# VectorE's extra work moved between a step's maxima and its masks, and the row sums' transpose moved one step earlier

## Chip, cores and metric

One core of a Trainium2 chip runs the whole kernel. The metric is the device time of one execution in microseconds, as the median of several runs.

## What is computed

Three layers in a row, on 2304 tokens (4 batches of 576) of width 512:

```python
scores = q @ k.T / sqrt(64)                       # 4 batches, 8 heads, 576 x 576
thresh = max(scores) - tau                        # per row
scores = where(scores >= thresh, scores, -1e9)
attn = exp(scores - max(scores)); attn /= sum(attn) + 1e-9
x = (attn @ v) as [2304, 512]
x = ((x @ w_a) * (x @ w_b)) @ w_out               # hidden width 1536; these weights come as float64
h = x @ w_in                                      # hidden width 1024, float64 too
out = layernorm(h * softmax(h)) * g_ln @ w_out2
```

## The kernel before

The kernel has three stages. `attention()` takes about the first 270 us of the trace, `moe1()` and `moe2()` the rest. The change is in `attention()` alone.

**Steps.** Two heads of a batch form a pair; there are 16 pairs. A pair has NS = 9 score tiles of 128 queries by 576 keys: eight for the two heads' four full query blocks, and a ninth for the last 64 queries of both. That makes 144 tiles, taken two at a time in 72 steps (`for m in range(tot // 2 + 6)`, line 474; the last six steps drain the pipeline). So a pair begins every four and a half steps. For each character of the string `PROG` (line 473) a step issues one piece of work. The order is written out by hand, and each engine takes its own instructions in the order in which they are issued:

- `A`, `B`: `score()` of the step's first and second tile. TensorE computes the scores into PSUM (line 332; two buffers `ps`). VectorE copies them out, negated and scaled, with their row maxima (line 337, "maxima" below). ScalarE takes the exponentials (line 349).
- `t`, `u`: the tile's threshold, a tiny operation of GpSimd (line 354).
- `V`: TensorE's products with the values (line 414).
- `F`: `finish()` of a pair. TensorE transposes the reciprocal row sums into PSUM (line 435, tile `rt`), and ScalarE copies them out (line 440, tile `zt`).
- `T`, `U`: transposes of the two tiles of the step before (line 383), which ScalarE copies out of PSUM (line 376).
- `Y`: transposes of last keys, that is of keys 512 to 575 (lines 399 and 402, tile `tq`). They exist only in two steps of a pair.
- `X`: in step 72 alone, the first products of the next stage.
- `a`, `b`: the masks of the two tiles, on VectorE (line 363). A mask needs the tile's exponentials and threshold.
- `f`, `z`: `fill()`, VectorE's extra work.

The tiles `rt`, `tp` (of `T` and `U`) and `tq` share one set of three PSUM buffers. A buffer is free when ScalarE has copied it out. ScalarE's copies are issued at the end of the step, behind the step's exponentials; those of `xp` and `zt` come first, then those of the transposes, then the conversion's.

**Extra work.** While attention runs, float64 weights are converted. A weight group has three pieces, and FW = 5 groups (15 pieces) may be converted before attention ends. A piece has six operations: an exponent on ScalarE (line 128); `low`, `sign` and `join` on VectorE (lines 132, 135, 138); a copy on ScalarE (line 142) and a difference on GpSimd (line 145). `fill()` issues one VectorE operation at a time; ScalarE's and GpSimd's are issued at the step's end (line 554). `conv_at` (line 472) lists the steps that may do this: the even ones from 6, and all from 72. If a pair's two operations on row sums (lines 369 and 370) are queued in `lo_old`, `fill()` takes these instead. From step 37, odd steps also issue one VectorE operation that prepares the next stage's input (`x_slots`, lines 228 and 234), eight in all.

Of the kernel before, what the change touches and what calls it, by code (L numbers as in the profile page):

```python
# [21 lines left out]
def kernel(  # L22
# [42 lines left out]
    NS = 2 * NQ + 1  # L65
# [83 lines left out]
    def conv_emit(stage, engs, count=1):  # L149
        while count and conv["k"] < min(conv["ld"], conv["lim"]):  # L150
            if not conv["ops"]:
                conv["ops"] = conv_ops(stage)
            if conv["ops"][0][0] not in engs:
                return
            conv["ops"].pop(0)[1]()
            count -= 1
            if not conv["ops"]:
                conv["k"] += 1
# [24 lines left out]
    def load_x(j):  # L183
        n = LEN[j]
        xr = xr_p.tile([P, KC, NB], F32, name="xr0")[:, :, 0:n]
        zr = xr_p.tile([P, KC, NB], F32, name="zr")[:, :, 0:n]
        for b, s0, m, c in BLK[j]:
            nc.sync.dma_start(out=xr[:, :, c:c + m], in_=xd[b][:, :, s0:s0 + m])
            if b not in vs:
                vs[b] = const.tile([P, KC, 2], F32, name=f"vs{b}")  # L190
                nc.sync.dma_start(out=vs[b], in_=xd[b][:, :, S:S + 2])
                vnew.append(b)
            for h in range(2):
                zs = rzd[b].rearrange("(k h) s -> h k s", h=2)[h:h + 1, :, s0:s0 + m]
                nc.sync.dma_start(out=zr[h * D:(h + 1) * D, :, c:c + m], in_=zs.to_broadcast([D, KC, m]))
        xs[j] = (xr, zr, xhs[j % 2].tile([P, KC, 2, NB], F32R, name="xt")[:, :, :, 0:n])
# [22 lines left out]
    def prep_slots(j):  # L219
        xr, zr, xt = xs[j]  # L220

        def norm(e):
            while vnew:
                b = vnew.pop()
                nc.vector.tensor_scalar(out=vs[b], in0=vs[b], scalar1=neg, scalar2=EPS / S, op0=ALU.mult, op1=ALU.mult)
            for b, _, m, o in BLK[j]:
                xe = xr[:, e, o:o + m]
                nc.vector.scalar_tensor_tensor(out=xe, in0=xe, scalar=vs[b][:, e, 0:1], in1=zr[:, e, o:o + m], op0=ALU.add, op1=ALU.mult)

        def high(e):  # L230
            nc.scalar.activation(out=xt[:, e, 0, :], in_=xr[:, e], func=AF.Copy)

        def low(e):
            nc.vector.tensor_tensor(out=xt[:, e, 1, :], in0=xr[:, e], in1=xt[:, e, 0, :].bitcast(F32), op=ALU.subtract)
            if e == KC - 1:
                later.append(lambda: nc.sync.dma_start(out=xsd[j], in_=xr))
                xs[j] = xt

        slots = []
        for c in range(0, KC, 2):  # L240
            slots += [(lambda e=e: norm(e), lambda e=e: high(e)) for e in range(c, c + 2)]
            slots += [(lambda e=e: low(e), None) for e in range(c, c + 2)]
        return slots
# [35 lines left out]
    def attention():  # L279
# [21 lines left out]
        def alloc_qk(i):  # L301
            q = pq.tile([P, 2, S], F32, name="q")
            k = pq.tile([P, 2, HS + D], F32, name="k")
            ld[i] = (q, k)
# [100 lines left out]
        def pv(i, r, half):  # L405
            n = R1 if r == 1 else R2 + 2
            if half == 0:
                st[i, "o", r] = ps_a.tile([P, 512], F32, name="po", bufs=1)
            po = st[i, "o", r][:, 0:n]
            vr, vt = ld[i, "v"], vz[i % 3]  # L410

            def mm(kc, h):
                lhsT, rhs = (vr[:, h * NQ + kc], dt[h, r][:, kc, 0:n]) if kc < NQ else (vt[:, h], dt["t", r][:, 0:n])
                nc.tensor.matmul(po[h * D:(h + 1) * D], lhsT=lhsT, rhs=rhs, start=(kc == 0), stop=(kc == NQ), skip_group_check=True)  # L414

            def store():
                b, hp = divmod(i, NPAIR)
                if r == 1:
                    st[i, "x"] = px.tile([P, S + 2], F32, name="xp")
                xp = st[i, "x"]  # L420
                c0 = 0 if r == 1 else R1
                nc.scalar.activation(out=xp[:, c0:c0 + n], in_=po, func=AF.Copy)
                if r == 2:
                    dma_q.append(lambda: nc.sync.dma_start(out=xd[b][:, hp, :], in_=xp))

            if half == 1:
                pv_q.append(store)
            cut = NQ // 2
            return [lambda kc=kc, h=h: mm(kc, h) for kc in (range(cut) if half == 0 else range(cut, NQ + 1)) for h in range(2)]
# [31 lines left out]
        tot = NP * NS  # L461

        def fill(n):
            for _ in range(n):
                if lo_old:
                    lo_old.pop(0)()
                elif m in conv_at:
                    conv_emit(wstage, "D")
                    if m >= tot // 2:
                        conv_emit(wstage, "APD", 2)  # L470

        conv_at = [x for x in range(6, tot // 2 + 6) if x % 2 == 0 or x >= tot // 2]
        PROG = 'ABtVFTUYXaufbz'
        for m in range(tot // 2 + 6):
            if m == 30:
                load_x(0)
                x_slots = prep_slots(0)
            cur = [divmod(n, NS) for n in (2 * m, 2 * m + 1) if n < tot]
            old = [divmod(n, NS) for n in (2 * m - 2, 2 * m - 1) if 0 <= n < tot]
            lo_old, lo_q = lo_q, []  # L480
            pvs = [(j,) + PV[j % 2][m - j * NS // 2] for j in range(max(0, 2 * m // NS - 2), min(NP, 2 * m // NS + 1)) if m - j * NS // 2 in PV[j % 2]]
            mms = [f for p in pvs for f in pv(*p)]
            nm = {}
            th = {}

            def score(k):
                if k < len(cur):
                    nm[k] = sm.tile([P, 1], F32, name="nm")
                    scores(*cur[k])
                    soft_max(*cur[k], nm[k])  # L490
                    soft_exp(*cur[k])

            def thr(k):
                if k < len(cur):
                    th[k] = soft_thr(nm[k])

            def mask(k):
                if k < len(cur):
                    soft_mask(*cur[k], th[k])
                    if cur[k][1] == NS - 1:  # L500
                        recip(cur[k][0])

            def turn(k):
                if k < len(old):
                    tpose(*old[k])

            for ch in PROG:
                if ch in "AB":
                    score("AB".index(ch))
                elif ch == "V":  # L510
                    for mm in mms:
                        mm()
                elif ch == "F":
                    for j in range(NP):
                        if m - j * NS // 2 == 9:
                            finish(j)
                elif ch in "TU":
                    turn("TU".index(ch))
                elif ch == "Y":
                    for c in old:  # L520
                        tpose_tail(*c)
                elif ch in "tu":
                    thr("tu".index(ch))
                elif ch in "ab":
                    mask("ab".index(ch))
                elif ch == "f":
                    fill(1)
                elif ch == "X":
                    if m == tot // 2:
                        pre[0, 0] = ab_mm(0, 0)  # L530
                elif ch == "z":
                    fill(max(1, len(lo_old)))
                    if m >= 37 and m % 2 and x_slots:
                        norm_low, high = x_slots.pop(0)
                        norm_low()
                        if high:
                            evac_q.append(high)
            for fn in dma_q + later:
                fn()
            dma_q.clear()  # L540
            later.clear()
            i, s = divmod(2 * m, NS)
            r = m - (i * NS + 1) // 2
            if i < NP and r == 0:
                load_v(i)
                if i + 2 < NP:
                    alloc_qk(i + 2)
                    load_k(i + 2)
                    load_q(i + 2)
            for fn in pv_q + evac_q:  # L550
                fn()
            evac_q, pv_q = [], []
            if m in conv_at:
                conv_emit(wstage, "AP", 3)
                conv_load(wstage)
# [300 lines left out]
```

## Time and profile before

| | us |
|---|---|
| median of 3 runs | 943.42 (943.14 to 944.04) |
| the profiled execution, its own time | 945.94 |
| its span, first to last instruction | 944.1 |

| engine | busy us | share of the span |
|---|---|---|
| TensorE, matmuls (PE) | 921.9 | 98% |
| TensorE, weight loads (PEld) | 704.0 | 75% |
| VectorE (DVE) | 542.4 | 57% |
| ScalarE (ACT) | 440.4 | 47% |
| GpSimd (POOL) | 192.6 | 20% |

The shares are means over three unlike stages. During attention VectorE and ScalarE are busy for 80 to 90% of the time, later for less than half. TensorE's matmuls are pipelined, and the ends of their rows are modelled, so that a busy TensorE may still have small gaps. TensorE's granted clock is full throughout.

### The profile page before, as it was taken

To read this page: it belongs to the slowest core of one execution; us is meant where nothing else is said; L and a number is where in the kernel's file an instruction comes from. 1 tells how busy PE (TensorE), PEld (TensorE's weight loads), DVE (VectorE), ACT (ScalarE), POOL (GpSimd) and SP (SyncE) were. 2 spreads that over 40 slices of the span, in tenths; PEclk is the share of its full clock that TensorE was granted. 3 is DMA by queue.
4 is the path that set the end of the run, shared out by engine and by line. 5 is a ranking of instruction groups with operands and counts; after the bars stand their busy time and mean duration, and the time that the engine had idled before them with its cause. 6 is when DMAs were issued, how large, how long until landed. Compare 5 with 4: busy or idle time off the path is not lost.

```text
span 944.1 us, 15070 instructions
## 1 busy us (share of the span) xinstructions
PE 921.9 (98%) x5680; PEld 704.0 (75%) x5680; DVE 542.4 (57%) x1169; ACT 440.4 (47%) x795; POOL 192.6 (20%) x292
## 2 busy tenths in 40 slices
PE   7999999999999999999999999999999999999998
PEld 3555555555567878889888888889988788888886
DVE  6898989999975754323147772222265544444443
ACT  5788887878763442213235432121232433333332
POOL 1111221212121220000013330000023433333330
PEclk9999999999999999999999999999999999999999
DMA  6443743463135474142115642022052111111100
GB/s 180 126 128 112 206 147 90 124 186 113 51 116 157 155 202 112 45 112 115 65 33 177 211 160 71 19 92 87 24 178 89 34 45 45 45 45 45 45 23 34
DMA packets 52616, 95.46 MB, mean 101 GB/s; under 512 B 12736, under 2 KB 28736, under 8 KB 49984
## 3 DMA queue, kind: packets, MB, share of 16 engines
q1 hardware_dynamic: 52112, 93.91, 32.1%
q8 instruction: 45, 0.74, 0.3%
q10 hardware_dynamic: 432, 0.59, 0.2%
q14 instruction: 27, 0.22, 0.1%
HBM read 70.80 MB, written 23.68 MB: 100 GB/s over the span
## 4 chain that ended last, share of the span: by engine, by line
PE 60%; DVE 3%; DMA 3%; ACT 2%; issue 1%; SPq 0%; POOL 0%; ACTq 0%; DVEq 0%
PE ps L256 26%; PE py L612 14%; PE po L754 10%; PE ps L698 9%; DMA wraw<-in_w_dram 2%; PE pl L735 2%; DVE g L596 1%; ACT gt L597 0%; DVE e L710 0%; DVE w L138 0%; ACT e L709 0%; DVE nm L706 0%; DVE xr L211 0%; ACT w L128 0%; ACT a L595 0%
## 5 line engine op out<-in xcount | busy, mean ns | idle before, releaser
L256 PE MATMUL ps<-xt,w 128*128 128x512 f32 (+1 forms) x1440 | 305.8, 368 | 1.9 <-DVE g L596 1.9
L256 PEld LDWEIGHTS ps<-xt,w 128*128 128x128 f32 x1440 | 251.4, 189 | 47.2 <-DVE g L596 2.3
L145 POOL TENSOR_TENSOR w<-w,w 128x512 fp32r<-128x512 f32 x52 | 76.8, 1478 | 413.5 <-ACT w L142 413.5
L612 PE MATMUL py<-gt,w 128*128 128x512 f32 (+1 forms) x720 | 157.5, 368 | 2.1 <-ACT y L616 2.1
L612 PEld LDWEIGHTS py<-gt,w 128*128 128x128 f32 x720 | 126.2, 189 | 25.0 <-ACT y L616 2.5
L596 DVE TENSOR_TENSOR g<-ps,a 128x512 f32<-128x512 f32 (+1 forms) x60 | 38.3, 638 | 180.7 <-ACT a L595 180.6
L349 ACT ACTIVATE pe<-ns,nm 128x576 f32<-128x576 f32 x128 | 94.0, 775 | 48.3 <-DVE ns L337 48.1
L595 ACT ACTIVATE a<-ps 128x512 f32<-128x512 f32 (+1 forms) x60 | 33.1, 552 | 178.2 <-PE ps L256 175.4
L363 DVE SCALAR_TENSOR_TENSOR pe<-ns,th,pe 128x576 f32<-128x576 f32 x128 | 102.7, 815 | 16.7 <-ACT pe L349 12.5
L337 DVE TENSOR_SCALAR_CACHE_REDUCE ns<-ps 128x576 f32<-128x576 f32 x144 | 102.7, 750 | 7.9 <-PE ps L332 7.8
L698 PE MATMUL ps<-w,ys 128*128 128x512 f32 x432 | 102.6, 393 | 1.6 <-POOL ys L575 1.4
L754 PE MATMUL po<-w,lt 128*128 128x512 f32 x432 | 101.4, 390 | 0.7 <-POOL lt L741 0.6
L332 PE MATMUL ps<-k,q 64*64 64x288 f32 x1152 | 91.2, 424 | 4.7 <-DMA k<-in_qkv_dram 4.4
L754 PEld LDWEIGHTS po<-w,lt 128*128 128x128 f32 x432 | 80.8, 188 | 18.1 <-POOL lt L741 1.1
L698 PEld LDWEIGHTS ps<-w,ys 128*128 128x128 f32 x432 | 79.8, 188 | 18.1 <-POOL ys L575 1.8
L414 PE MATMUL po<-pt,vr 128*64 128x322 f32 (+1 forms) x512 | 78.0, 419 | 1.7 <-ACT pt L376 0.9
L376 ACT ACTIVATE pt<-tp 128x512 f32<-128x512 f32 (+1 forms) x160 | 77.9, 545 | 0.2
L354 POOL TENSOR_SCALAR th<-nm,toff 128x1 f32<-128x1 f32 x144 | 38.4, 269 | 187.8 <-DVE ns L337 187.8
L383 PEld LDWEIGHTS tp<-ident,pe 128*128 128x128 f32 x512 | 55.9, 141 | 24.9 <-issue 9.4
L383 PE MATMUL tp<-ident,pe 128*128 128x128 f32 x512 | 70.9, 278 | 1.1 <-ACT pt L376 0.6
L414 PEld LDWEIGHTS po<-pt,vr 128*64 128x64 f32 x512 | 32.7, 136 | 42.5 <-issue 17.2
L332 PEld LDWEIGHTS ps<-k,q 64*64 64x64 f32 x1152 | 36.8, 134 | 32.8 <-DVE ns L337 7.8
(76 smaller groups left out, 807.6 us busy)
## 6 DMA issues: line engine op xcount, KB each, us to landing
wraw<-in_w_dram SPq DMA_DIRECT2D x36, 512.0 KB, 3.7
q<-in_qkv_dram SPq DMA_DIRECT2D x15, 576.0 KB, 4.1
k<-in_qkv_dram SPq DMA_DIRECT2D x30, 176.0 KB, 4.7
xd<-xp SPq DMA_DIRECT2D x16, 289.0 KB, 2.1
y<-yd SPq DMA_DIRECT2D x18, 256.0 KB, 3.0
vr<-in_v_dram SPq DMA_DIRECT2D x16, 256.0 KB, 3.7
xr<-xd SPq DMA_DIRECT2D x4, 1024.0 KB
zr<-rzd SPq DMA_DIRECT2D x8, 512.0 KB, 9.5
```

The lines of the kernel that those rows point to most:

```text
L145: nc.gpsimd.tensor_tensor(out=w["o"][1], in0=w["f"] if wide else raw, in1=w["o"][0].bitcast(F32), op=ALU.subtract)
L256: nc.tensor.matmul(pa[:, 0:n], lhsT=wt[:, m, wi, kc * P:(kc + 1) * P], rhs=xt[:, kc, xi, :], start=(k == 0), stop=(k == 3 * KC - 1))
L332: nc.tensor.matmul(ps[t * D:(t + 1) * D, g, 0:HS], lhsT=q[r, u, c], rhs=k[r, u, o:o + HS], start=True, stop=True, skip_group_check=True)
L337: nc.vector.tensor_scalar(out=ns, in0=st[i, s][:, :, 0:HS], scalar1=-SCALE, scalar2=None, op0=ALU.mult, op1=ALU.min, accum_out=nm)
L349: nc.scalar.activation(out=pe.rearrange("p (g s) -> p g s", g=2), in_=ns, func=AF.Exp, bias=nm, scale=-1.0)
L363: nc.vector.scalar_tensor_tensor(out=pv, in0=ns, scalar=th, in1=pv, op0=ALU.is_le, op1=ALU.mult, accum_out=z[:, s:s + 1])
L376: evac_q.append(lambda: nc.scalar.activation(out=out, in_=in_, func=AF.Copy))
L383: nc.tensor.transpose(tp[:, kc, :], pe[:, o:o + P], ident)
L414: nc.tensor.matmul(po[h * D:(h + 1) * D], lhsT=lhsT, rhs=rhs, start=(kc == 0), stop=(kc == NQ), skip_group_check=True)
L612: nc.tensor.matmul(py, lhsT=wt[:, 2, wi, oc * P:(oc + 1) * P], rhs=gt[:, gi, :], start=(first and k == 0), stop=(last and k == 2))
L698: nc.tensor.matmul(ph[:, g, :], lhsT=y[:, a, kc, :], rhs=w2(2 * kc + g, b), start=(k == 0), stop=(k == 3 * KC - 1))
L754: nc.tensor.matmul(po, lhsT=lt[:, a, j, :], rhs=w2(2 * KC + j, b), start=(k == 0), stop=(k == 3 * NJ - 1))
```

## The change

The thresholds `t` and `u` are issued together, ahead of `V`. The order `a` `u` `f` `b` `z` at the step's end becomes `f` `a` `b`: one place for VectorE's extra work, after both maxima and ahead of both masks. There a step issues all that is queued on row sums, and then one operation more: the preparation of the next stage's input where it has one, else one of the conversion. Conversion is allowed in every step from 6. `finish()` runs 8 steps after its pair began, and not 9.

```diff
-        conv_at = [x for x in range(6, tot // 2 + 6) if x % 2 == 0 or x >= tot // 2]
-        PROG = 'ABtVFTUYXaufbz'
+        conv_at = range(6, tot // 2 + 6)
+        PROG = 'ABtuVFTUYXfab'
...
                     for j in range(NP):
-                        if m - j * NS // 2 == 9:
+                        if m - j * NS // 2 == 8:
                             finish(j)
...
-                elif ch == "f":
-                    fill(1)
...
-                elif ch == "z":
-                    fill(max(1, len(lo_old)))
+                elif ch == "f":
+                    fill(len(lo_old))
                     if m >= 37 and m % 2 and x_slots:
                         norm_low, high = x_slots.pop(0)
                         norm_low()
                         if high:
                             evac_q.append(high)
+                    else:
+                        fill(1)
```

## Rows read from the trace of the kernel before

**Rows 1.** Page, section 1: busy us of each engine over the whole span.
```profile
PE 921.9 (98%) x5680; PEld 704.0 (75%) x5680; DVE 542.4 (57%) x1169; ACT 440.4 (47%) x795; POOL 192.6 (20%) x292
```

**Rows 2.** Steps 7 to 70: length, then busy us of PE, PEld, DVE, ACT, POOL; clock.
```profile
30.05:266.97 236.92, 231.12 (x2237) 134.07 (x2236) 215.22 (x587) 191.43 (x371) 47.57 (x139) 1.00 0.43 128
```

**Rows 3.** Timeline (start us, length us), VectorE, steps 65 and 66.
```profile
246.13 0.75 DVE L337 TENSOR_SCALAR_CACHE_REDUCE ns<-ps 128x576 f32<-128x576 f32 x1
...
246.81 0.75 DVE L337 TENSOR_SCALAR_CACHE_REDUCE ns<-ps 128x576 f32<-128x576 f32 x1
...
247.81 0.82 DVE L363 SCALAR_TENSOR_TENSOR pe<-ns,th,pe 128x576 f32<-128x576 f32 x1 [0.23 <-POOL th L354]
...
249.29 0.76 DVE L337 TENSOR_SCALAR_CACHE_REDUCE ns<-ps 128x576 f32<-128x576 f32 x1
...
251.72 0.42 DVE L132 TENSOR_SCALAR wlow<-wraw 128x512 uint32<-128x512 uint32 x1
252.05 0.81 DVE L363 SCALAR_TENSOR_TENSOR pe<-ns,th,pe 128x576 f32<-128x576 f32 x1
...
252.79 0.80 DVE L135 SCALAR_TENSOR_TENSOR wlow<-wraw,wlow 128x512 uint32<-128x512 uint32 x1
253.51 0.75 DVE L337 TENSOR_SCALAR_CACHE_REDUCE ns<-ps 128x576 f32<-128x576 f32 x1
```

**Rows 4.** Timeline, TensorE's matmuls, in step 63 and in step 65.
```profile
239.48 0.60 PE L383 MATMUL tp<-ident,pet 128*128 128x128 f32 x4
240.95 0.44 PE L399 MATMUL tq<-ident,pe 128*128 128x128 f32 x2 [0.87 <-ACT zt L440]
...
246.11 1.09 PE L383 MATMUL tp<-ident,pe 128*128 128x128 f32 x8
247.04 0.38 PE L399 MATMUL tq<-ident,pe 128*128 128x128 f32 x2
247.35 1.20 PE L332 MATMUL ps<-k,q 64*64 64x288 f32 x16
```

**Rows 5.** Waits from 27 to 272 us: total us, times, longest.
```profile
DVE pe L363 <- ACT pe L349: 11.5, 49, 0.2
...
PEld tq L399 <- ACT zt L440: 5.5, 6, 1.6
...
PEld ps L332 <- DVE ns L337: 4.8, 18, 0.5
DVE ns L337 <- PE ps L332: 4.8, 7, 0.7
...
PE tq L399 <- ACT zt L440: 4.1, 5, 1.4
```

**Rows 6.** Timeline, TensorE's weight loads ahead of the value products, steps 51 and 67.
```profile
193.51 1.01 PEld L414 LDWEIGHTS po<-pt,vr 128*64 128x64 f32 x8 [1.11 <-ACT pt L376]
...
252.41 0.63 PEld L414 LDWEIGHTS po<-pt,vr 128*64 128x64 f32 x8 [0.44 <-ACT pt L376]
```

**Rows 7.** Groups of VectorE's instructions from 27 to 272 us: busy us, mean ns.
```profile
L138 DVE SCALAR_TENSOR_TENSOR w<-w,wlow 128x512 uint32<-128x512 uint32 x12 | 8.2, 687 | 0.0
...
L370 DVE RECIPROCAL rz<-rz 128x9 f32<-128x9 f32 x16 | 3.4, 210 | 0.0
L228 DVE SCALAR_TENSOR_TENSOR xr<-xr,vs,zr 128x512 f32<-128x512 f32 x4 | 2.9, 735 | 0.0
```

**Rows 8.** Timeline: GpSimd's differences and VectorE's operations near them.
```profile
246.22 1.29 POOL L145 TENSOR_TENSOR w<-w,w 128x512 fp32r<-128x512 f32 x1 [1.98 <-ACT w L142]
...
266.97 0.76 DVE L337 TENSOR_SCALAR_CACHE_REDUCE ns<-ps 128x576 f32<-128x576 f32 x1
267.66 1.28 POOL L145 TENSOR_TENSOR w<-w,w 128x512 fp32r<-128x512 f32 x1 [2.67 <-ACT w L142]
...
276.61 1.30 POOL L145 TENSOR_TENSOR w<-w,w 128x512 fp32r<-128x512 f32 x1 [1.29 <-ACT w L142]
276.73 1.47 DVE L132 TENSOR_SCALAR wlow<-wraw 128x512 uint32<-128x512 uint32 x1 [0.86 <-DMA wraw<-in_w_dram]
```

**Rows 9.** Timeline, ScalarE's first copy of the stage after attention.
```profile
284.39 0.60 ACT L595 ACTIVATE a<-ps 128x512 f32<-128x512 f32 x1 [2.79 <-DMA rzd<-zt]
```

## The prediction

> **What bounds the kernel now.** I read the busy totals first. TensorE is at 98% of the span [rows 1], but a mean over three stages settles nothing, so I took the stretch that the change touches, from the first maximum of step 7 to that of step 71: 236.92 us for 64 steps, 3.70 us each [rows 2]. VectorE is busy for 215.22 us of it (91%), ScalarE for 191.43 (81%). TensorE's matmuls cover 231.12 us, which leaves only 5.80 uncovered. Two engines look full, and the question is which one waits for the other.
>
> The timelines answer it. VectorE runs its queue end to end, except for one gap per step: between the second maximum and the first mask it waits for the exponentials of the first tile, or for its threshold. With an operation every 0.68 us the second maximum of step 65 makes room at 247.49; the mask starts at 247.81, 0.32 later [rows 3]. The waits show the same: 49 masks waited for exponentials [rows 5]. TensorE also runs end to end: in an ordinary step transposes, last keys and the next scores follow at 246.11, 247.04 and 247.35, and no step has slack between its blocks beyond a constant 0.1 us or so [rows 4]. VectorE waited for scores only 7 times, 4.8 us in all [rows 5]. So the two are balanced within a few microseconds, and **whatever VectorE saves, TensorE gives at most the time that it loses today**. That is the core of the forecast.
>
> What TensorE loses is of three kinds:
> - In six steps that hold both `F` and `Y` (18, 27 and so on, every ninth; step 9 has none) four tiles want three PSUM buffers, and `tq` waits for the copy `zt`, which stands on ScalarE behind the step's exponentials. In step 63 the last group of four transposes starts at 239.48; at 0.11 us each (eight take from 246.11 to 247.04, with their start) `tq` would have started at 239.92 and started at 240.95: 1.03 lost [rows 4]. The same subtraction in all six steps gives 0.18, 1.03, 0.51, 1.53, 0.82 and 1.03, together 5.1. The waits by name bracket it: 4.1 on matmuls and 5.5 on weight loads [rows 5].
> - In five steps between 37 and 51, where odd steps hold extra work besides the even ones' conversion, VectorE falls behind, ScalarE's copies come late, and the value products wait for them: 1.11 us in step 51 where an ordinary step shows 0.44 of unavoidable turn-around [rows 6]. The excess of the five is 0.67, 0.49, 0.38, 0.37 and 0.11, together 2.0.
> - Scores that wait for VectorE to empty `ps` show 18 small waits [rows 5]; beyond the ordinary spacing some 0.45 is lost.
>
> Together 7.6 us; the ceiling of the gain.
>
> **The change, part by part.**
>
> *`finish()` one step earlier.* With 9 the row sums' transpose falls on last keys in every second pair; with 8 the steps are 8, 12, 17, 21, ..., and last keys are in 2, 5, 7, 9, 11, 14, 16, 18, ...: never together. Its matmul and copy stay. The reciprocals are ready, since `lo_old` issues them five steps after a pair began. Last keys without row sums show no wait: the eight transposes from 246.11 are followed at once [rows 4]. So 5.1 us go, between 4.1 and 5.5. On SP's queue the pair's two small stores now stand ahead of the loads of steps 9, 18, ... and no longer ahead of those of 14, 23, ...; these loads are for a pair that begins nine steps later, so either order is covered.
>
> *Extra work ahead of the masks.* An operation there runs inside the 0.32 us gap. A step without extra work takes 246.13 to 249.29, 3.16; less the gap 2.84. Conversion costs 0.33 for `low` (252.05 minus 251.72), 0.72 for `sign` (253.51 minus 252.79) [rows 3] and about 0.6 for `join` (0.687 less the 0.08 by which neighbours overlap), the input's operations about 0.65, a pair's two on row sums 0.2 [rows 7]. The smallest still fills the gap. So each step that holds one saves 0.32 on VectorE. They are 15 pieces of three operations and 8 input operations, one per step from 8: steps 8 to 60, 53 steps, 17 us. Against that, three pieces that were converted after step 71 (the trace has 12 joins by then [rows 7]) now lie inside, 3 x 1.65 = 5.0. For steps 7 to 70 VectorE then needs 53 x 2.84 = 150.5, conversion 15 x 1.65 = 24.8, input 8 x 0.65 = 5.2, row sums 14 x 0.2 = 2.8, and 11 steps without extra work 34.8: 218.1 us, where TensorE needs 236.92 - 7.6 = 229.3. VectorE drops out as a bound, and the second and third kinds of wait (2.45) go too.
>
> *What it may cost.* GpSimd's difference for a piece runs right after its `join` step. Today it overlaps only the next step's maxima, and these are not stretched: it starts at 246.22 in step 65 and ends 1.38 after the first maximum; the latest of 12 ends 1.97 after it [rows 8]. The maxima end after 1.36, so VectorE never meets it with anything else. Now `low` of the next piece, or an input operation, stands just there. A `low` that starts while a difference runs takes 1.47 us in place of 0.42: 276.73, ending 0.29 after the difference [rows 8]. Call the delay D per piece. From the 12 rows as they are it would be 0 to 0.6; as the step before is now shorter (`join` inside the gap), I add 0.2 and take D = 0.4, 6 us in all, with 0 and 1.6 (a whole difference, 1.30, and 0.3 for the threshold that queues behind it on GpSimd) as ends. VectorE then needs 218.1 + 6 = 224.1, under TensorE's 229.3. But in steps 8 to 60 alone it has only (150.5 + 24.8 + 5.2 + 2.4 + 6) / 53 = 3.56 us a step against 3.58, so a late mask or copy will now and then show. I leave 0.8 us for that, between nothing and the 2.45 of today.
>
> The Trainium skill has the rule behind those rows ("SBUF — State Buffer", section "SBUF: two separate sides"): VectorE and GpSimd share a port pair as an exclusive lock, and the loser blocks for the whole instruction. It speaks against this change; the 1.47 agrees with it, and the unstretched maxima, which read PSUM, fit too.
>
> *Threshold `u` earlier.* GpSimd issues nothing between `t` and `u` in either order; nothing.
>
> *ScalarE.* Three pieces more, about 1.3 us each, on 191.43 of 236.92 [rows 2]: hidden, and if ever late it shows in the 0.8 above.
>
> *After attention.* The last pair's products, `finish()` and the stores keep their order, and the next stage's first copy waits for the store of `zt` [rows 9], as now. Everything behind shifts with TensorE. Conversions that leave the drain steps free nothing there, as TensorE runs without a gap from 272 on, past that copy.
>
> **Sum.** 5.1 + 2.0 + 0.45 - 0.8 = 6.75. The profiled span 944.1 becomes 937.4 (1.84 us lie outside it, and stay); the median 943.42 becomes 936.7.
>
> **Rivals.**
> - *VectorE was the bound.* For it: 91% busy, end to end. Then the gain is its own balance, 17.0 - 5.0 + 4.8 of waits for scores = 16.8: 926.6. Against it: TensorE has only 5.80 us uncovered. The Trainium skill ("Perfetto Trace Analysis", section "Identifying the Most-Contended Engine") judges TensorE by weight loads, not by matmul time; these are 134.07 of 236.92, 57%, which would make VectorE the most contended engine. The spacing of the blocks says otherwise, and I follow it. Chance 4%.
> - *The lock takes VectorE's saving.* If D is about 1.2, VectorE needs 218.1 + 18 = 236.1 in the 236.92: no change, 942 to 943. Chance 8%.
> - *The lock costs more than it gives.* From D = 1.25 on VectorE's sum passes today's 236.92. At D = 1.6 it is 242.1, 5.2 more: 948.6. It would take differences that start about a microsecond later against the maxima than in the 12 rows, as when ScalarE's queue grows. Chance 5%.
> - *Only part arrives:* `finish()` helps, but late copies cost the 2.45 and more: a gain of 2 to 4, 940.4. Chance 8%.
>
> **How the numbers follow.** The forecast, a gain of 4 to 8.5, has 75%, 936.7 its middle. The range takes all of the ceiling and 1.3 for the bounds below, 934.5, and reaches to a gain of 2 above, 941.4. A measurement tells 0.2% (1.9 us) from no change. Faster: 75 + 8 + 4 = 87, less one for gains under 1.9: 0.86. Same: 0.09. Slower: 0.05.
>
> **What would show it.** After: no wait of `tq` for `zt`; uncovered TensorE time in attention under 2 us; the 0.32 gap gone from steps 8 to 60 and still there from 61; VectorE waiting for scores more often than 7 times; `low` near 1 us wherever a difference overlaps it. I am wrong if the distance from first maximum to first scores of the next stage shrinks by under 4 us, or if TensorE's waits name VectorE.

## The result and the profile after

| | kernel before | changed kernel |
|---|---|---|
| median, us (6 runs each) | 944.84 (943.14 to 946.51) | 936.58 (935.89 to 939.82) |
| profiled execution, its own time | 945.94 | 939.82 |
| span | 944.1 | 938.0 |
| first maximum of step 7 to that of step 71 | 236.92 | 230.09 |

The ratio is 0.9915, 95% interval 0.9899 to 0.9931: 8.0 us faster, between 6.5 and 9.5. The forecast was 936.7, a gain of 6.75.

The stretch of steps 7 to 70 in the changed kernel, to be laid beside [rows 2] (length, then busy us of PE, PEld, DVE, ACT and POOL):

```profile
29.80:259.89 230.09, 229.44 (x2240) 133.73 (x2236) 221.78 (x596) 193.39 (x377) 68.52 (x143) 1.00 0.45 136
```

It lost 6.83 us, and TensorE's uncovered time went from 5.80 to 0.65. VectorE's busy time rose by 6.6 us: more of the conversion lies in the stretch, and operations are delayed behind GpSimd. GpSimd's rose by 21 us: four differences more lie in the stretch (5.2 us), and its 128 thresholds take 50.0 us in place of 33.9; many of them now run beside VectorE's extra work, and the longest takes 0.81 us.

TensorE's timeline in step 63, beside the first two of [rows 4]:

```profile
233.55 0.60 PE L383 MATMUL tp<-ident,pet 128*128 128x128 f32 x4
233.99 0.38 PE L399 MATMUL tq<-ident,pe 128*128 128x128 f32 x2
```

From 1.47 us between the two starts to 0.44: the wait is gone, and no wait of `tq` for `zt` is left. The waits from 27 to 265 us that answer to [rows 5] (total us, times, longest):

```profile
PEld ps L332 <- DVE ns L337: 5.6, 23, 0.5
...
PEld tp L383 <- DVE pe L363: 4.1, 9, 0.5
DVE ns L337 <- PE ps L332: 3.6, 6, 0.9
...
DVE pe L363 <- ACT pe L349: 2.1, 9, 0.2
DVE pe L363 <- POOL th L354: 2.0, 10, 0.5
```

Masks wait for exponentials 9 times instead of 49. VectorE does not wait for scores more often than before (6 times, before 7), and TensorE's weight loads still wait for VectorE: 5.6 us for maxima, where it was 4.8, and 4.1 us for masks. VectorE has not dropped out as a bound; it is level with TensorE.

Step 35 on VectorE, GpSimd and ScalarE, a step right behind a `join`:

```profile
130.31 0.74 DVE L337 TENSOR_SCALAR_CACHE_REDUCE ns<-ps 128x576 f32<-128x576 f32 x1
130.55 0.66 ACT L142 ACTIVATE w<-w 128x512 fp32r<-128x512 f32 x1
...
131.28 1.28 POOL L145 TENSOR_TENSOR w<-w,w 128x512 fp32r<-128x512 f32 x1 [2.25 <-ACT w L142]
131.66 1.18 DVE L132 TENSOR_SCALAR wlow<-wraw 128x512 uint32<-128x512 uint32 x1
131.70 0.79 ACT L349 ACTIVATE pe<-ns,nm 128x576 f32<-128x576 f32 x1
...
132.55 0.67 POOL L354 TENSOR_SCALAR th<-nm,toff 128x1 f32<-128x1 f32 x2
133.02 0.82 DVE L363 SCALAR_TENSOR_TENSOR pe<-ns,th,pe 128x576 f32<-128x576 f32 x1 [0.17 <-POOL th L354]
...
134.50 0.75 DVE L337 TENSOR_SCALAR_CACHE_REDUCE ns<-ps 128x576 f32<-128x576 f32 x1
```

`low` meets the difference and takes 1.18 us in place of 0.42. The threshold stands behind the same difference, and the mask waits another 0.17 us for it. ScalarE's exponentials start late here too, since the copy and the next exponent stand before them, but the first ends by 132.49 and `low` only at 132.84, so the mask does not wait for them. The step takes 4.19 us, where TensorE's mean is 3.6. In steps 8 to 60 ten masks wait in this way, each for a threshold right behind a difference, 1.7 us in all; none there waits for exponentials. The groups of VectorE's extra work from 30 to 260 us (busy us, mean ns) give the delay, beside [rows 7]:

```profile
L132 DVE TENSOR_SCALAR wlow<-wraw 128x512 uint32<-128x512 uint32 x15 | 10.0, 668 | 0.0
...
L228 DVE SCALAR_TENSOR_TENSOR xr<-xr,vs,zr 128x512 f32<-128x512 f32 x4 | 3.3, 826 | 0.0
L234 DVE TENSOR_TENSOR xt<-xr,xt 128x512 fp32r<-128x512 f32 x4 | 3.2, 808 | 0.0
L369 DVE TENSOR_SCALAR rz<-z 128x9 f32<-128x9 f32 x14 | 3.1, 221 | 0.0
L370 DVE RECIPROCAL rz<-rz 128x9 f32<-128x9 f32 x14 | 3.0, 216 | 0.5
```

15 x (0.668 - 0.412) + 4 x (0.826 - 0.735) + 4 x (0.808 - 0.673) = 4.7 us, 0.31 a piece (0.412 is the mean without the delay, from the run with the copy ahead of copies below; 0.735 and 0.673 are the means in the kernel before). With the 1.7 us of the masks it is 6.4 us, 0.43 a piece.

The last two rows show a cost that the prediction had counted too low. In the kernel before, a mask stood between a pair's two operations on row sums, and the two took 0.20 us a pair from start to start. Now the second stands right behind the first, whose result it needs, and they take 0.33 to 0.63 us a pair, 5.4 us in all.

Behind attention the two profiled executions differ as well. TensorE waits for a weight piece, 3.44 us here and 1.88 before, and here its granted clock then falls. The changed kernel, then the kernel before, in 25 us about this wait (columns as above; the last but two is the granted clock):

```profile
285.00:310.00 25.00, 21.56 (x89) 17.37 (x88) 13.53 (x19) 7.64 (x12) 2.88 (x2) 0.93 0.66 179
```

```profile
292.00:317.00 25.00, 23.12 (x103) 18.81 (x102) 14.30 (x21) 8.05 (x13) 2.88 (x2) 1.00 0.64 178
```

And in the changed kernel's timeline:

```profile
297.37 0.68 ACT L128 ACTIVATE w<-wraw 128x512 f32<-128x512 f32 x1 [7.30 <-DMA wraw<-in_w_dram]
...
299.32 7.22 PE L256 MATMUL ps<-xt,w 128*128 128x512 f32 x24 [3.44 <-DVE g L596]
```

These 24 matmuls take 7.22 us, and the granted clock is 0.51 from 299.32 to 302.60; the 24 ahead of the wait take 5.60. The wait varies between executions of one and the same kernel: it was 3.44, 4.13 and 2.55 us in three of the changed kernel. Whether the change has a part in it is not shown. So steps 7 to 70 are the sharper measure: the same three executions gave 230.09, 229.99 and 230.28.

### The profile page after: what moved, and what is told of

The parts are those of the page before. It is cut to its first block, busy times and chain, and to the rows that moved or that the text cites. A ratio compares the mean times of both kernels' runs of the same rounds, so it can differ in the third digit from the quotient of the medians.

```text
span 938.0 us, 15035 instructions
## 1 busy us (share of the span) xinstructions
PE 921.9 (98%) x5680; PEld 706.0 (75%) x5680; DVE 541.5 (58%) x1169; ACT 438.0 (47%) x795; POOL 208.2 (22%) x292
## 4 chain that ended last, share of the span: by engine, by line
PE 76%; DVE 14%; issue 4%; ACT 3%; DMA 2%; POOL 1%; SPq 0%; ACTq 0%; DVEq 0%; POOLq 0%
PE ps L256 30%; PE py L612 15%; PE ps L698 10%; PE po L754 10%; DVE ns L337 6%; DVE pe L363 4%; PE po L414 3%; PE ps L332 3%; PE tp L383 3%; PE pl L735 2%; DMA wraw<-in_w_dram 1%; ACT pe L349 1%; DVE pet L363 1%; ACT pt L376 1%; POOL th L354 0%
## 5 line engine op out<-in xcount | busy, mean ns | idle before, releaser
L363 DVE SCALAR_TENSOR_TENSOR pe<-ns,th,pe 128x576 f32<-128x576 f32 x128 | 100.2, 813 | 5.0 <-ACT pe L349 2.8
L354 POOL TENSOR_SCALAR th<-nm,toff 128x1 f32<-128x1 f32 x144 | 54.3, 380 | 158.5 <-DVE ns L337 153.5
```

Source lines behind the costliest of these rows:

```text
L363: nc.vector.scalar_tensor_tensor(out=pv, in0=ns, scalar=th, in1=pv, op0=ALU.is_le, op1=ALU.mult, accum_out=z[:, s:s + 1])
```

## The experiments

| kernel | time, ratio to before (95%) | steps 7 to 70 |
|---|---|---|
| before | 1 | 236.92 |
| changed, second and third time | 0.9921 (0.9900 to 0.9941), 0.9931 (0.9903 to 0.9958) | 229.99, 230.28 |
| `finish()` moved alone | 0.9974 (0.9955 to 0.9994) | 233.48 |
| extra work moved alone | 0.9953 (0.9939 to 0.9967) | 232.10 |
| no lock | 0.9899 (0.9881 to 0.9917) | 227.01 |
| short `sign` | 0.9902 (0.9877 to 0.9927) | 227.56 |
| fewer value products | 0.9862 (0.9842 to 0.9882) | 227.10 |
| later load of the input | 0.9939 (0.9915 to 0.9963) | 230.13 |
| copy ahead of copies, twice | 0.9904 (0.9878 to 0.9931), 0.9900 (0.9874 to 0.9927) | 227.20, 227.20 |
| the same, and input loaded in step 60 | 0.9854 (0.9827 to 0.9880) | 227.20 |
| no lock, `finish()` at 9 | one execution, 938.01 us | 229.08 |

**The changed kernel again**, as the yardstick of two groups.

> The changed kernel once more, as the yardstick of this group of runs. Theory (TensorE bounds attention once its waits are gone): about 8 us under the kernel before, as first measured (936.58 against 944.84); first maximum of step 7 to first maximum of step 71 about 230 us.

> The changed kernel as the yardstick of this group. Steps 7 to 70 again 230 us, the time again some 7.5 us under the kernel before; the rest of the difference between executions lies after attention, where TensorE waits for weight pieces.

The stretch came out so both times. The times were 938.87 and 940.29 us beside 946.10 and 944.64 for the kernel before, 7.2 and 4.4 us less; the second falls short of the forecast.

**`finish()` alone**, in the kernel before.

```diff
-                        if m - j * NS // 2 == 9:
+                        if m - j * NS // 2 == 8:
```

> The kernel before with finish() 8 steps after its pair began, and nothing else. Theory (two engines in balance): the wait of tq for zt (5.1 us in six steps) goes, but VectorE without its 4.8 us of waits for scores still needs 232.1 us for steps 7 to 70, so the stretch falls from 236.9 to 232 to 233.5 and the time by 3.5 to 4.8 us. Rival (the parts simply add): 5.1 us. Rival (VectorE's new place brings it all): no change, within 1 us.

```profile
30.18:263.66 233.48, 230.85 (x2236) 133.76 (x2232) 214.59 (x586) 191.34 (x370) 47.56 (x139) 1.00 0.42 129
```

The stretch falls by 3.44, at the far end of what balance gave; the 5.1 of the waits do not arrive. The time falls by 0.26% (0.06 to 0.45%), 2.5 us, less than the 3.5 to 4.8 expected. Weight loads of scores now wait for VectorE 8.0 us in place of 4.8. The parts don't simply add, and this part is not nothing.

**Extra work alone**: the changed kernel with `finish()` at 9.

```diff
-                        if m - j * NS // 2 == 8:
+                        if m - j * NS // 2 == 9:
```

> The changed kernel with finish() back at 9 steps. Theory (the wait for zt is long because ScalarE's exponentials run late behind VectorE, so an earlier VectorE shortens it): the six waits shrink from 5.1 us to some 1.2, as in step 9, where VectorE had not yet fallen behind and 0 to 0.2 was lost; the gain is about 5.5 us against the kernel before. Rival (each part mends its own waits, and they add): the 5.1 stay, the gain is 2 to 3 us.

Its waits by name, to lay beside [rows 5]:

```profile
PEld tq L399 <- ACT zt L440: 4.7, 6, 1.1
...
PE tq L399 <- ACT zt L440: 3.2, 5, 0.8
```

The stretch is 232.10, a gain of 4.8; the theory asked for 5.5, the rival for 2 to 3. But the reason given was wrong. The waits for `zt` did not shrink to 1.2: by the starts of the matmuls they cost 4.2, against 5.1. Most of the gain came from other waits: those ahead of the value products (2.0 us) are gone, and those of the scores and between the value products, which I had counted too low or not at all, fell from 2.6 to 0.5. Its steps 26 and 27, where the wait for `zt` is 1.0 us:

```profile
100.20 1.18 DVE L132 TENSOR_SCALAR wlow<-wraw 128x512 uint32<-128x512 uint32 x1
...
103.82 1.45 ACT L349 ACTIVATE pe<-ns,nm 128x576 f32<-128x576 f32 x2 [1.08 <-DVE ns L337]
...
105.44 0.25 ACT L440 ACTIVATE zt<-rt 9x128 f32<-9x128 f32 x1
```

`low` is held up in step 26. In step 27 ScalarE stands idle for 1.08 us until the maxima come, and `zt` has its place behind the exponentials of these maxima. So here `zt` is late because VectorE is.

**No lock.** The changed kernel, with zeros written in place of the difference for the 15 pieces.

```diff
+            if k < 3 * FW:
+                nc.gpsimd.memset(w["o"][1].bitcast(F32), 0.0)
+                return
             nc.gpsimd.tensor_tensor(out=w["o"][1], in0=w["f"] if wide ...
```

> The changed kernel; for the 15 pieces converted in attention GpSimd writes zeros with a memset in place of the difference of two tensors (the low parts of these weights are left out). Theory (TensorE bounds, the delay of VectorE behind GpSimd is hidden): low and the input operations return to their undelayed lengths (0.42 and 0.65 to 0.75), VectorE saves the 5.6 us that the delays sum to, and the time stays within 1 us of the changed kernel. Rival (VectorE bounds after the change): 4 to 5.6 us faster than the changed kernel.

```profile
29.82:256.83 227.01, 227.01 (x2240) 133.63 (x2236) 216.65 (x596) 194.64 (x377) 56.39 (x143) 1.00 0.45 138
```

`low` is back at 0.41 us each (6.2 us for 15). The zeros need not wait for ScalarE's copy. They are written right behind `join`, in 0.53 us, and 3 us ahead of the next `low`:

```profile
127.45 0.53 POOL L146 MEMSET w<- 128x512 f32 x1
```

So this run takes the meeting of the two engines away; what a memset beside a `low` would cost it does not show. The stretch falls by 3.0, the time by 2.3 us (936.58 beside 938.87), to neither of the two forecasts: part of the delay was on the path. And this run shows TensorE's own need: no matmul starts later than its kind allows anywhere from step 7 to 70, no time is uncovered, and that takes 227.0 us.

**Short `sign`**, sparing VectorE some 7 us and leaving the lock alone.

```diff
-            nc.vector.scalar_tensor_tensor(out=w["l"], in0=raw[:, :, 1], ..., in1=w["l"], ...)
+            u = 64 if k < 3 * FW else n
+            nc.vector.scalar_tensor_tensor(out=w["l"][:, 0:u], in0=raw[:, 0:u, 1], ..., in1=w["l"][:, 0:u], ...)
```

> The changed kernel; in the 15 pieces converted in attention VectorE's sign operation covers 64 of 512 columns (the signs of the other columns of these weights are left out). VectorE is spared about 0.5 us a piece, 7.5 us in all; the delay behind GpSimd stays. Theory after the run without the lock (TensorE's own need for steps 7 to 70 is 227.0 us, and the 3.0 above it in the changed kernel come from the steps in which GpSimd holds VectorE up): the stretch falls from 230.0 by 0.5 to 1.5 us only, since VectorE merely catches up sooner after such a step. Rival (VectorE's total bounds): down to 227.0, by 3 us, as without the lock.

```profile
29.55:257.11 227.56, 227.56 (x2240) 133.70 (x2236) 215.61 (x596) 194.46 (x377) 63.86 (x143) 1.00 0.44 138
```

The rival was nearer. Either relief of VectorE brings TensorE to within 0.6 us of its own need. So the 3.0 us hang on VectorE's sum, of which the lock is one term.

**Fewer value products**, sparing TensorE work.

```diff
-        return [... for kc in (range(cut) if half == 0 else range(cut, NQ + 1)) for h in range(2)]
+        return [... for kc in (range(1) if half == 0 else range(cut, NQ + 1)) for h in range(2)]
```

> The changed kernel without the value products of one of the five key blocks (keys 128 to 255 are left out of both heads' sums). TensorE is spared 0.216 and 0.27 us twice a pair, about 0.48 us, 7 us in steps 7 to 70; its own need falls from 227.0 to 220. Theory (TensorE bounds with VectorE close behind): the stretch falls by 3 to 5 us, to 225 to 227, where VectorE's 222 us of work and its delays behind GpSimd take over. Rival (VectorE bounds already): no change, within 0.5 us. Rival (TensorE alone, with room on VectorE): 7 us.

```profile
29.69:256.79 227.10, 221.12 (x2122) 124.67 (x2118) 221.43 (x595) 192.47 (x376) 69.53 (x143) 1.00 0.45 138
```

What TensorE is spared was expected at half its size. A block of value products and the transposes behind it, in the changed kernel and then here:

```profile
108.00 1.31 PE L414 MATMUL po<-pt,vr 128*64 128x322 f32 x8
109.23 1.09 PE L383 MATMUL tp<-ident,pe 128*128 128x128 f32 x8
```

```profile
106.90 0.76 PE L414 MATMUL po<-pt,vr 128*64 128x322 f32 x4
107.60 0.66 PE L383 MATMUL tp<-ident,pe 128*128 128x128 f32 x4
```

From start to start that is 1.23 and 0.70 us, 0.53 less; a block of 256 columns loses 0.43. A pair has one of each, so TensorE is spared 0.96 us a pair, some 14 us in the stretch, and its own need falls to about 213. Yet the stretch falls by 3 us only. Of the 14 us that TensorE has to spare, busy time shows 6 as uncovered. So VectorE, with what it waits for, needs 227.1 us in the changed kernel. Both engines need 227; together they take 230.

**Copy ahead of copies.** ScalarE's copy of a joined piece is issued first at the step's end, and all work is done.

```diff
+            if m in conv_at and conv["ops"] and len(conv["ops"]) == 2:
+                conv_emit(wstage, "A")
             for fn in pv_q + evac_q:
                 fn()
```

> The changed kernel; ScalarE's copy of a joined piece is issued ahead of the step's copies out of PSUM, so that GpSimd's difference starts about 1 us earlier and ends before VectorE's next extra operation. All work is done. Theory (the lock's delay, not the difference itself, costs the 3.0 us above TensorE's need): low returns to 0.42 us in most steps and the stretch falls from 230.0 to 227.5 to 229. Rival (the copies out of PSUM are now late by 0.63 us and TensorE waits for them): no change or slower, 230 to 232.

> The changed kernel with ScalarE's copy of a joined piece ahead of the copies out of PSUM, beside the changed kernel on one chip. Theory (TensorE has no wait left in attention): steps 7 to 70 again 227.2 us, 2.9 under the changed kernel, and the time 2 to 4 us under it. Rival (what is won in attention is lost again to the weight loads after it): within 1 us.

Step 34 and what follows, on ScalarE, VectorE and GpSimd:

```profile
127.75 0.61 ACT L142 ACTIVATE w<-w 128x512 fp32r<-128x512 f32 x1
128.31 0.81 DVE L363 SCALAR_TENSOR_TENSOR pe<-ns,th,pe 128x576 f32<-128x576 f32 x1
128.45 1.81 POOL L145 TENSOR_TENSOR w<-w,w 128x512 fp32r<-128x512 f32 x1 [0.68 <-ACT w L142]
...
130.85 0.42 DVE L132 TENSOR_SCALAR wlow<-wraw 128x512 uint32<-128x512 uint32 x1
```

The difference now runs into the second mask and is itself held up, 1.81 us in place of 1.28, which nobody waits for; it ends at 130.26, and `low` finds the way free. 227.20 us, twice, just under what was expected: within 0.2 us of TensorE's own need, with all the work in place. The copies out of PSUM are later by 0.6 us, and no wait shows it. On one chip beside the changed kernel the time is 936.07 against 940.29, 4.2 us less.

**Later load of the input.**

```diff
-                if n == 0:
+                if n == 1:
                     load_x(1)
```

> The changed kernel; load_x(1), 2 MB of input for the stage after attention, is issued after the stage's second unit and not after its first, so that a weight piece's load no longer stands behind it. Theory (the gap of 3.8 us of TensorE at 295.5 us is this piece's load, 11.35 us to landing): the gap falls under 1 us and the granted clock does not fall behind it; 3 to 5 us faster than the changed kernel. Rival (the input is then what lands late): the gap moves by one or two units and nothing is gained.

The rival held. The gap at 295 us is gone, but TensorE's weight loads wait 1.35 us at 304 and 3.8 us at 335 (0.93 and 3.41 between the matmuls); the time is no better.

**Input loaded in step 60**, on top of the copy ahead of copies.

```diff
             if m == 30:
                 load_x(0)
                 x_slots = prep_slots(0)
+            if m == 60:
+                load_x_in(1)          # the DMAs of load_x(1) alone
```

> As the run before, and the second batch's input (2 MB) is loaded in step 60 of attention and not after the next stage's first unit. Theory (the gap of TensorE behind attention is a weight piece's load that queues behind this input): the gap near 292 us goes, and the granted clock with it stays up; 2 to 4 us more, some 6 us under the changed kernel. Rival (the weight piece is late in any case, as in the run with the later load): the gap only moves to a later unit, within 1 us of the run before.

```profile
285.04 5.60 PE L265 MATMUL ps<-xt,w 128*128 128x512 f32 x24
...
290.48 2.88 PE L625 MATMUL py<-gt,w 128*128 128x512 f32 x12
293.20 5.60 PE L265 MATMUL ps<-xt,w 128*128 128x512 f32 x24
```

TensorE now runs through where it had waited for 2.55 to 4.13 us in the changed kernel. The time is 931.90 us, 4.2 under the run before and 8.4 under the changed kernel on that chip, a little more than expected, and its runs lie within 0.3 us (931.67 to 931.94). It is the fastest of all that ran with the whole computation.

**No lock, `finish()` at 9.** The kernel without the lock with the one line of the second experiment.

> The kernel without the lock (GpSimd writes zeros in place of the difference for the 15 pieces of attention; their low parts are left out) and finish() back at 9 steps. Theory now (with the extra work at its new place the wait of tq for zt stays near 4 us because the lock and the late exponentials of the step before delay zt): without the lock the six waits shrink to about 2 us, the stretch is 229. Rival (zt stands behind two exponentials whatever VectorE does): about 1 us in each of six or seven steps, the stretch 232 to 233.

```profile
PEld tq L402 <- ACT zt L443: 2.1, 5, 0.5
...
PE tq L402 <- ACT zt L443: 0.9, 4, 0.2
```

229.08, as the theory had it: with the lock gone the same waits cost 1.8 us (by the starts of the matmuls) in place of 4.2. So more than half of the lateness of `zt` came from the meetings of VectorE and GpSimd; that the rest comes from its place behind two exponentials is likely, but not shown apart.

## Why the prediction was right, by its own steps

**TensorE is what gives, and at most what it loses.** Right, and shown: the 17 us that the forecast saved on VectorE brought 6.83, and of TensorE's uncovered time 0.65 was left. The rival by which VectorE alone was the bound (a gain of 16.8) fell with it.

**VectorE drops out as a bound.** Wrong, and two of the prediction's own signs say so: VectorE waits for scores 6 times and not more often than 7, and TensorE's weight loads name VectorE. The other signs came out: no wait for `zt`, 0.65 us uncovered, a stretch shorter by 6.83, the gap ahead of the mask gone from step 8 to 60 but for the waits for thresholds. `low` is near 1 us in five of the eight meetings with a difference and at 0.58 in three.

**The ceiling, 7.6.** Too small. TensorE's own need is 227.0, so the ceiling was 9.9. Summed from start to start of the matmuls against the run without the lock, the waits for `zt` and what directly follows were 5.1 + 0.3, those ahead of the value products 2.0 and those of the scores 0.8. Some 1.8 I had not counted: waits between value products of one block, which look like a wider spacing of the matmuls and not like a gap.

**The rest that stays, 0.8.** Too small as well: 3.0. It sits within transposes (0.9), within scores (0.9), ahead of the products (0.6) and between them (0.6). The step that failed is the sum of VectorE's own need: 224.1 by my terms, 227.1 as the run with fewer products shows. From start to start of VectorE's operations in that run, a pair's operations on row sums take 5.3 us in all where 2.8 were counted, `low` and the input's operations with their delays 17.6 for 16.2, and 1.4 us, mostly waits for scores, were not counted at all; against that, `sign` and `join` take 18.0 for 19.8, and the gaps that stay 3.1 for 3.5. Late exponentials are no part of it. That two engines with equal needs of 227 take 230 together stood in the sum only as the 0.8. The two errors cancel: 9.9 - 3.0 = 6.9, where 7.6 - 0.8 = 6.8 was forecast. That the size came out so close is luck; the mechanism, waits of TensorE that go, is not.

**`finish()`, 5.1 alone.** The waits went, but alone it brought 3.4, and the extra work alone 4.8; together 6.8. Neither is the sum of the waits that it names, since a wait that goes lets the other engine's lateness show.

**Extra work in the gap.** As forecast: of 49 waits for exponentials 9 are left, none of them in steps 8 to 60, and the smallest operation fills the gap.

**The lock.** D was taken as 0.4, the threshold's wait included, and measured 0.43 in the mean: 0.31 in VectorE's operations (up to 0.77 where `low` is hit in full) and the rest in masks that wait for thresholds. The Trainium skill's rule ("SBUF — State Buffer", section "SBUF: two separate sides"), that the side that starts first keeps the ports for the whole instruction, agrees with the traces in both directions: `low` takes 1.18 us against 0.42 where it starts under a difference, and the difference 1.81 against 1.28 where it starts under a mask.

**Threshold, ScalarE, drain.** No run takes the threshold's earlier issue apart; thresholds as such became longer (0.39 us in the mean, before 0.27). ScalarE's load was hidden but for late copies, the 0.6 ahead of the products. What the conversions that left the drain steps changed behind attention was not tested by itself.

**The size of 8.0 against 6.83.** The rest lies outside steps 7 to 70, where executions differ by more than that; its cause isn't settled by these runs. That 936.58 lies so near the forecast 936.7 is chance in part: the kernel before stood at 943.42 when the forecast was made and at 944.84 in the comparison.

## What to carry to other kernels

Where two engines both run end to end, find each one's own need by sparing the other (here 227.0 and 227.1): here the stretch took 3 us more than either need, and a saving on one engine was worth no more than what the other lost. Read waits on TensorE from the distances between the starts of its matmuls, kind by kind; busy time hides the short ones (before, 5.80 us were uncovered where 9.9 were lost). A filler placed in an engine's gap meets what its neighbours do at that moment, and moving the neighbour as well (one copy, 1.5 us earlier behind its `join`) was worth another 2.9 us.

An operation can also become dearer by its new neighbours alone, as the row sums' two did when they came to stand one behind the other.

## What the runs showed of the hardware

A GpSimd operation of two tensors took 1.81 us in place of 1.28 when it started under a VectorE mask, and VectorE's `low` took up to 1.19 us in place of 0.41 when it started under such an operation. GpSimd's thresholds, of one column, took 0.39 us in the mean in the changed kernel and 0.27 before.

After TensorE's wait of 3.44 us at 295 to 299 us the granted clock fell to its lower level (0.51 from 299.32 to 302.60: 1.2 GHz in place of 2.4), and 24 matmuls took 7.22 us in place of 5.60. The length of the wait alone does not decide it. The same place with the extra work moved alone, and then in the kernel before:

```profile
299.97 7.38 PE L256 MATMUL ps<-xt,w 128*128 128x512 f32 x24 [1.87 <-DVE g L596]
```

```profile
304.83 5.74 PE L256 MATMUL ps<-xt,w 128*128 128x512 f32 x24 [1.88 <-DVE g L596]
```

After waits of 1.79 us (the second run of the copy ahead of copies) and 1.89 (no lock) the 24 took 7.35 and 7.36 us, after one of 1.99 (short `sign`) 5.74. Where the clock fell, the wait cost 1.6 to 1.8 us more than its own length, and 2.5 us after the longest, of 4.13 us.
